# Reordering block 0's transposes and fill-in products in a fused attention and FFN kernel

## The chip, the cores and the metric

The kernel runs on one NeuronCore of a Trainium2 chip. The metric is the device time of one execution in microseconds (us), and the time of a kernel is the median over its runs. A profile of one execution comes with it: its times count from the start of the span, the stretch from the first to the last instruction.

The engines are named as in the profile: PE does matrix products and transposes (PEld is its weight loads), DVE and ACT are the vector and the scalar engine, POOL and SP here mostly issue transfers. PE writes only PSUM, which has eight banks of 128 x 512 fp32; ACT and DVE copy from there to SBUF.

## The reference

Linear ("lightning") attention with a decay for each head, followed by a gated FFN on its output. There are 4 batches, 8 heads, 768 positions and a head width of 64; d_model is 512, d_ff 1536.

```python
for b in range(nb):                                   # blocks of 64 positions
    intra = einsum('bhic,bhjc->bhij', qb, kb) * Dmask
    intra = einsum('bhij,bhjd->bhid', intra, vb)
    inter = einsum('bhid,bhde->bhie', qb * lam_pow, kv_state)
    out[:, :, sl] = intra + inter
    kv_state = lam_block * kv_state + einsum('bhsd,bhse->bhde', kb * rev_pow, vb)
x = out as (batch * seq, heads * head_dim)
y = (sigmoid(x @ w_gate) * (x @ w_val)) @ w_out
```

## The kernel before

The sequence is cut into six blocks of 128 positions, numbered n = 0 to 5. For each block the attention of all four batches gives `XT` (d_model by 512 tokens, bf16), and the FFN runs over it: `gp` and `vp` (L553) are the gate and value products, twelve tiles of d_ff each, `po` (L585) the output product. All matrix operands are bf16. In the steady part the attention of block n+1 is slipped between the FFN's products of block n by a written plan (`plan`, L672 on). The schedule is manual: each engine runs its instructions in the order in which the program lists them.

The change lies in block 0, which has no earlier FFN to hide behind. It has no incoming state, so its attention is scores, mask and output alone. Its list stands at L601 to L636. For each batch b:

- `t_0("k", b)` and `t_0("q", b)` (L285) transpose k and q on PE, eight small transposes each, into a PSUM tile `tk` or `tq`. For batches 0 and 1, k comes as fp32 (`h`) by two early loads and is cast on DVE (`cast_hw`, L358); everything else is loaded with a cast by POOL's queue.
- `e_k` (L353) and `e_q` (L340) copy these tiles to SBUF as `KS` and `QS`. ACT makes all the copies but that of `QS` of batch 0, which is DVE's.
- `s_0(b)` (L295) makes the scores in two PSUM banks `sp`, sixteen matmuls of 64 x 64 weights by 128 columns; DVE multiplies each bank with the decay mask (`MT`, L302), so there are eight such operations in all.
- `a_0(b)` (L311) multiplies with v into a bank `op`, and ACT copies it to `XT` (L318); for batch 3 the bank is split in two halves, and ACT and DVE copy one each.

The FFN's first products of tile 0 are taken in two halves (batches 0 and 1, then 2 and 3), so that they may start on the first half of `XT`.

Between these steps stand fill-in products, `zeros(m)` (L599): m matmuls of a zeroed tile with itself, 512 bf16 columns each, into a bank `zps` that nobody reads. There are eleven ahead of the first transpose and ten in between.

PSUM is shared by two pools: `ps_at` (five banks, tag "ps") for attention and `ps_ff` (three, tag "ff") for the FFN. A pool hands its banks round in turn, so a new tile waits until the last reader of the bank's tile of before is done. In the list before, each batch's `tk` and `tq` has a bank of its own, and `tk` of batches 2 and 3 lies in the FFN's pool, which also holds `zps`.

Of the kernel before, what the change touches and what calls it, by code (L numbers as in the profile page):

```python
# [8 lines left out]
FP32 = mybir.dt.float32  # L9
BF16 = mybir.dt.bfloat16  # L10
AF = mybir.ActivationFunctionType
ALU = mybir.AluOpType
# [4 lines left out]
def kernel(  # L17
# [11 lines left out]
    nc = tc.nc  # L29

    B, H, S, D = q.shape
    C = 128
    NSTEP = S // C
    HP = H // 2
    DM = H * D
# [11 lines left out]
    trsb = ctx.enter_context(tc.tile_pool(name="trsb", bufs=3))  # L47
# [6 lines left out]
    ps_at = ctx.enter_context(tc.tile_pool(name="ps_at", bufs=5, space=bass.MemoryType.PSUM))  # L54
    ps_ff = ctx.enter_context(tc.tile_pool(name="ps_ff", bufs=3, space=bass.MemoryType.PSUM))
# [19 lines left out]
    def swapped(n, b):  # L75
        return n > 0 and b >= NB2
# [7 lines left out]
    def rows_of(u):  # L84
        return slice(u * 64, (u + 1) * 64)
# [67 lines left out]
    ST, CP, XD = {}, {}, {}  # L153
# [50 lines left out]
    lamq, lamqs = lamq2[:, 0], lamq2[:, 1]  # L204
# [15 lines left out]
    def powers(w):  # L220
        nc.scalar.activation(mask0[:, w], mask0[:, w], AF.Exp)
# [47 lines left out]
    QS, KS, MT, XT, SP, OP = {}, {}, {}, {}, {}, {}  # L269
    QT, KT = {}, {}  # L270
    tqs, tks = {}, {}
# [5 lines left out]
                nc.tensor.transpose(ps[:, i, hp, :], T_[c, n][:, b, 2 * hp:2 * hp + 2, :], ident)  # L277
        (tqs if c == "q" else tks)[n, bs[0]] = ps

    def t_0(c, b, pool=ps_at, tag="ps"):  # L280
        ps = pool.tile([128, 1, HP, C], BF16, name="t" + c, tag=tag)
        for a in range(2):
            for e in range(2):
                for w in range(2):
                    nc.tensor.transpose(ps[rows_of(w), 0, 2 * a + e, :],  # L285
                                        T_[c, 0][:, b, 2 * (2 * a + w) + e, :], ident)
        (tqs if c == "q" else tks)[0, b] = ps

    def s_0(b):
        sp = [ps_at.tile([128, HP, C], FP32, name=f"sp{w}", tag="ps") for w in range(2)]  # L290
        for a in range(2):
            for e in range(2):
                for w in range(2):
                    for g in range(2):
                        nc.tensor.matmul(sp[w][rows_of(g), 2 * a + e, :],  # L295
                                         lhsT=KS[0, b][rows_of(w), 2 * a + e, rows_of(g)],
                                         rhs=QS[0, b][rows_of(w), 2 * a:2 * a + 2, rows_of(g)],
                                         start=(a == 0 and e == 0), stop=(a == 1 and e == 1),
                                         skip_group_check=True)
        MT[0, b] = mtp.tile([128, 2, HP, C], BF16, tag="MT", name="MT")  # L300
        for w in range(2):
            nc.vector.tensor_tensor(out=MT[0, b][:, w], in0=sp[w], in1=mask0[:, w], op=ALU.mult)  # L302

    def a_0(b, engs):
        n = len(engs)
        ops = [ps_at.tile([128, HP // n, C], FP32, name="op", tag="ps") for _ in range(n)]
        for r in range(HP):
            for e in range(2):
                for g in range(2):
                    o, i = divmod(r, HP // n)  # L310
                    nc.tensor.matmul(ops[o][rows_of(g), i, :], lhsT=T_["v", 0][rows_of(g), b, 2 * r + e, :],  # L311
                                     rhs=MT[0, b][rows_of(g), r % 2, 2 * (r // 2) + e, :],
                                     start=(i == 0 and e == 0), stop=(i == HP // n - 1 and e == 1),
                                     skip_group_check=True)
        if b == 0:
            new_xt(0)
        for o, eng in enumerate(engs):
            (eng.tensor_copy if eng is nc.vector else eng.copy)(  # L318
                XT[0][:, b // 2, o * (HP // n):(o + 1) * (HP // n), b % 2 * C:(b % 2 + 1) * C], ops[o])
# [12 lines left out]
        for bp in range(2):  # L332
            nc.scalar.copy(ST[1, 0][:, bp], cp[bp])

    def e_q(n, bs, eng=None):
        w = len(bs)
        src = tqs[n, bs[0]] if n < FIRST_XBAR else QT[n][:, bs[0]:bs[0] + w]
        t = trsb.tile([128, 2, HP, C], BF16, tag="QS", name="QS")
        if n == 0:
            (nc.scalar.copy if eng is nc.scalar else nc.vector.tensor_copy)(t[:, :w], src)  # L340
        else:
            nc.vector.tensor_tensor(
                out=t[:, :w], in0=src,
                in1=(lamqs if swapped(n, bs[0]) else lamq).unsqueeze(1).to_broadcast([128, w, HP, C]),
                op=ALU.mult)
        for i in range(w):
            QS[n, bs[i]] = t[:, i]

    def e_k(n, bs, parts=1):
        t = trsb.tile([128, 2, HP, C], BF16, tag="KS", name="KS")  # L350
        w = len(bs) // parts
        for i in range(parts):
            nc.scalar.copy(t[:, i * w:(i + 1) * w], tks[n, bs[0]][:, i * w:(i + 1) * w])  # L353
        for i in range(len(bs)):
            KS[n, bs[i]] = t[:, i]

    def cast_hw(b):
        nc.vector.tensor_copy(T_["k", 0][:, b], H32[:, b])  # L358
# [52 lines left out]
    def new_xt(n):  # L411
        XT[n] = xtp.tile([128, 2, NMT, TCH // 2], BF16, tag="XT", name="XT")
# [181 lines left out]

    zps = ps_ff.tile([128, DM], FP32, name="zps", tag="ff")

    def zeros(m):
        for _ in range(m):
            nc.tensor.matmul(zps, lhsT=ST[1, 0][:, 0, 0], rhs=ST[1, 0][:, 0], start=True, stop=True)  # L599

    exponents(0)  # L601
    powers(0)
    exponents(1)
    powers(1)
    zeros(11)
    cast_hw(0)
    cast_hw(1)
    t_0("k", 0)
    e_k(0, [0])
    zeros(1)  # L610
    t_0("k", 1)
    t_0("q", 0)
    e_q(0, [0], nc.vector)
    e_k(0, [1])
    t_0("q", 1)
    e_q(0, [1], nc.scalar)
    zeros(1)
    s_0(0)
    zeros(1)
    s_0(1)  # L620
    for b in range(2, 4):
        t_0("k", b, ps_ff, "ff")
        e_k(0, [b])
    zeros(3)
    for b in range(2, 4):
        t_0("q", b)
        e_q(0, [b], nc.scalar)
    zeros(1)
    s_0(2)
    a_0(0, (nc.scalar,))  # L630
    s_0(3)
    a_0(1, (nc.scalar,))
    zeros(2)
    a_0(2, (nc.scalar,))
    zeros(1)
    a_0(3, (nc.scalar, nc.vector))  # L636


# [183 lines left out]
```

## Time and profile before

| | |
|---|---|
| median of 4 runs | 225.37 us (225.08 to 225.67) |
| the profiled execution | 225.08 us, span 223.3 us |
| PE busy in the span | 216.8 us (97%) |
| DVE, ACT, POOL busy | 103.2, 108.6, 63.5 us |
| PE busy, 0 to 6.66 us | 4.77 of 6.66 |
| PE busy, 6.66 to 9.50 us | 2.58 of 2.84 |
| PE busy, 9.50 to 15.66 us | 5.44 of 6.16 |
| PE busy, 15.66 us to the end | 204.01 of 207.64 |

A line of the timeline gives the start in us, the busy time, the engine, the line of the kernel, the operation, what it writes and reads, the shape, the count, and in brackets the idle time of the engine before it with what ended it. The chain of waits follows the work that ended last back from the last instruction. Ends of matmuls are modelled, so their starts are the better measure; and a few matmul records can be missing (the page counts 18 fill-in products where the list has 21). A fill-in product counts as busy like any other.

### The profile page before, as it was taken

What the parts mean: (1) busy time and instruction counts of PE and PEld (TensorE: products, weight loads), DVE (VectorE), ACT (ScalarE), POOL (GpSimd) and SP (SyncE); (2) the same over time, 40 slices, a digit from 0 to 9 for tenths busy, and PEclk for the clock granted to TensorE, in tenths of its full rate; (3) what the DMA queues carried; (4) which work ended last, traced back from release to release, by engine and by line L of the source; (5) the groups of instructions that cost most, each with busy time, mean ns of one, the idle gap of its engine ahead of it and who ended that gap; (6) DMA issues with size and microseconds to landing.
All of it is one profiled execution on the core that took longest, in us unless ns stands there. A gap on an engine that the chain in (4) does not pass through costs nothing.

```text
span 223.3 us, 5470 instructions
## 1 busy us (share of the span) xinstructions
PE 216.8 (97%) x2310; PEld 107.7 (48%) x2321; DVE 103.2 (46%) x191; ACT 108.6 (49%) x237; POOL 63.5 (28%) x85
## 2 busy tenths in 40 slices
PE   7889999999999999999999999999999999999994
PEld 2565444557444544444544444544444544444443
DVE  4754565539777600785700686700676400333300
ACT  5757764494384523385433376342366342333221
POOL 7999855740291009302920030000000000000000
PEclk9999999999999999999999999999999999999999
DMA  6999999999899999997999986012100012100022
GB/s 116 175 179 187 196 199 183 165 156 167 127 96 157 267 217 120 175 132 163 95 158 178 234 58 41 3 50 94 47 3 0 3 48 96 47 0 1 3 94 95
DMA packets 99401, 25.27 MB, mean 113 GB/s; under 512 B 90032, under 2 KB 96432, under 8 KB 99376
## 3 DMA queue, kind: packets, MB, share of 16 engines
q0 software_dynamic: 77872, 13.90, 77.8%
q1 hardware_dynamic: 20688, 10.69, 19.4%
q10 hardware_dynamic: 816, 0.33, 0.6%
q8 instruction: 18, 0.29, 0.5%
q14 instruction: 7, 0.06, 0.1%
HBM read 28.32 MB, written 6.29 MB: 155 GB/s over the span
## 4 chain that ended last, share of the span: by engine, by line
PE 95%; DMA 2%; issue 1%; DVE 1%; ACT 0%; ACTq 0%; DVEq 0%
PE gp L553 28%; PE po L585 28%; PE vp L553 28%; DMA h<-in_k_dram 2%; PE sp L449 1%; PE cp L509 1%; PE op L473 1%; PE op L487 1%; PE zps L599 1%; PE op L311 1%; PE tk L285 1%; PE sp L295 1%; PE sp L375 0%; PE op L406 0%; PE tq L277 0%
## 5 line engine op out<-in xcount | busy, mean ns | idle before, releaser
L543 DVE SCALAR_TENSOR_TENSOR ht<-sg,vp 128x512 bf16<-128x512 f32 x72 | 49.5, 687 | 93.3 <-PE vp L553 88.5
L553 PE MATMUL gp<-XT,WG 128*128 128x512 bf16 (+1 forms) x296 | 74.3, 374 | 0.0
L553 PE MATMUL vp<-XT,WV 128*128 128x512 bf16 (+1 forms) x296 | 74.3, 373 | 0.0
L563 ACT ACTIVATE sg<-gp 128x512 f32<-128x512 f32 x72 | 43.0, 597 | 59.2 <-PE gp L553 59.2
L585 PE MATMUL po<-WO,ht 128*128 128x512 bf16 (+2 forms) x292 | 63.5, 370 | 0.7 <-issue 0.2
L553 PEld LDWEIGHTS <-WV 128*128 128x128 bf16 x296 | 29.0, 98 | 33.2
L585 PEld LDWEIGHTS <-ht 128*128 128x128 bf16 x300 | 28.2, 98 | 32.2 <-issue 0.4
L553 PEld LDWEIGHTS <-WG 128*128 128x128 bf16 x296 | 28.2, 98 | 31.3
L589 ACT ACTIVATE ob<-po 128x512 f32<-128x512 f32 (+1 forms) x24 | 14.0, 583 | 38.9 <-PE po L585 38.9
L143 ACT ACTIVATE kd<-kb,kds 128x128 bf16<-128x128 bf16 x80 | 25.2, 390 | 0.0
L661 POOL COPY gates<-qt 128x1 bf16<-128x1 bf16 x4 | 0.7, 186 | 50.2 <-DMA qt<-qb 50.2
L499 ACT CAST XT<-op 128x512 bf16<-128x512 f32 x16 | 8.2, 599 | 5.0 <-PE op L487 5.0
L459 DVE TENSOR_TENSOR MT<-sp,mask 128x512 bf16<-128x512 f32 x16 | 10.3, 682 | 0.0
L96 POOL DMA_DIRECT2D vb<-in_v_dram x6 | 9.0, 1501 | 3.2 <-issue 1.6
L102 POOL DMA_DIRECT2D qb<-in_q_dram x10 | 8.8, 893 | 3.2 <-DMA WO<-in_moe_w_out_dram 3.2
L102 POOL DMA_DIRECT2D kb<-in_k_dram x10 | 9.0, 920 | 1.0 <-DMA WG<-in_moe_w_gate_dram 0.5
L599 PE MATMUL zps<-st 128*128 128x512 bf16 x18 | 7.1, 530 | 1.7 <-DVE st L174 1.5
L121 POOL DMA_DIRECT2D WV<-in_moe_w_val_dram x9 | 7.4, 840 | 0.3 <-DMA WG<-in_moe_w_gate_dram 0.3
L118 POOL DMA_DIRECT2D WG<-in_moe_w_gate_dram x8 | 6.8, 856 | 0.0
L534 DVE SCALAR_TENSOR_TENSOR st<-st,pow_l,cp 128x128 bf16<-128x128 bf16 x24 | 6.7, 342 | 0.0
L96 POOL DMA_DIRECT2D kb<-in_k_dram x5 | 5.9, 1185 | 0.9 <-DMA WG<-in_moe_w_gate_dram 0.9
L353 ACT COPY KS<-tk 128x512 bf16<-128x512 bf16 (+1 forms) x6 | 4.3, 728 | 3.6 <-PE tk L277 2.1
(91 smaller groups left out, 126.7 us busy)
## 6 DMA issues: line engine op xcount, KB each, us to landing
out_dram<-ob SPq DMA_DIRECT2D x19, 256.0 KB, 2.0
vb<-in_v_dram POOLq DMA_DIRECT2D x4, 512.0 KB, 7.2
qb<-in_q_dram POOLq DMA_DIRECT2D x14, 128.0 KB, 7.6
kb<-in_k_dram POOLq DMA_DIRECT2D x12, 128.0 KB, 9.0
WO<-in_moe_w_out_dram POOLq DMA_DIRECT2D x4, 384.0 KB, 12.0
kb<-in_k_dram POOLq DMA_DIRECT2D x5, 256.0 KB, 9.4
qb<-in_q_dram POOLq DMA_DIRECT2D x5, 256.0 KB, 9.1
WG<-in_moe_w_gate_dram POOLq DMA_DIRECT2D x4, 256.0 KB, 7.0
```

The costliest lines, as they stand in the source:

```text
L96: nc.gpsimd.dma_start(out=T_[c, n][:, b0:nat], in_=src[b0:nat, :, sl, :].rearrange("b h s d -> s (b h) d"))
L102: nc.gpsimd.dma_start(out=T_[c, n][:, m:b1, u::2, :], in_=src[m:b1, 1 - u::2, sl, :].rearrange("b h s d -> s (b h) d"))
L121: nc.gpsimd.dma_start(out=WV[:, :, f0 * 128:f1 * 128], in_=wv_r[:, :, f0 * 128:f1 * 128])
L143: nc.scalar.mul(KD[n][:, at, i, :], T_["k", n][:, at, i, :], kds[:, min(n // FIRST_XBAR, 1), h:h + 1])
L459: nc.vector.tensor_tensor(out=MT[n, bp][:, u], in0=SP[n, bp][u], in1=mask[:, u ^ bp].unsqueeze(1).to_broadcast([128, 2, HP, L]), op=ALU.mult)
L499: nc.scalar.copy(XT[n][:, bp].rearrange("p m (j c i) -> p m j c i", j=2, c=2)[:, :, :, c, :], OP[n, c, bp])
L543: return nc.vector.scalar_tensor_tensor(out=o, in0=g, scalar=1.0, in1=x, op0=ALU.add, op1=ALU.mult)
L553: nc.tensor.matmul(ps[:, part], lhsT=W[:, mt, fs], rhs=XT[n][:, part, mt], start=(part is not second and mt == 0), stop=(part is not first ...
L563: nc.scalar.activation(sg, gp.rearrange("p a b -> p (a b)"), AF.Tanh, scale=0.5)
L585: nc.tensor.matmul(po[:, :c1 - c0], lhsT=HT[n, ft][:, tt * 128:(tt + 1) * 128], rhs=WO[:, ft, c0:c1], start=(ft == 0), stop=(ft == NFT - 1))
L589: (eng.mul if eng is nc.scalar else eng.tensor_scalar_mul)(o, po[:, :c1 - c0], 0.5)
L599: nc.tensor.matmul(zps, lhsT=ST[1, 0][:, 0, 0], rhs=ST[1, 0][:, 0], start=True, stop=True)
```

## The change

- q of a batch is transposed right behind its k: in the list k0, q0, k1, q1, where k0, k1, q0, q1 stood.
- The transposed k of two batches share one PSUM bank, one half each, and so do the transposed q. All of them lie in `ps_at`.
- The copies of block 0 have a function of their own, `e_0`. DVE copies `QS` of batches 0 and 1, ACT the rest.
- For batches 2 and 3 the order is k2, k3, q2, scores 2, q3, output 0, scores 3, output 1; q3 stood ahead of scores 2.
- The outputs of batches 0 and 1 go to banks of the FFN's pool.
- The fill-in products read the same zeroed tile as fp32. Three of 512 columns stand at the start, where eleven were; one of 384 ahead of q2 and one of 256 behind it; the others are gone.

```diff
-    def t_0(c, b, pool=ps_at, tag="ps"):
-        ps = pool.tile([128, 1, HP, C], BF16, name="t" + c, tag=tag)
+    def t_0(c, b):
+        ts = tqs if c == "q" else tks
+        if b % 2 == 0:
+            ts[0, b] = ps_at.tile([128, 2, HP, C], BF16, name="t" + c, tag="ps")
+        ps = ts[0, b & ~1]
         for a in range(2):
             for e in range(2):
                 for w in range(2):
-                    nc.tensor.transpose(ps[rows_of(w), 0, 2 * a + e, :],
+                    nc.tensor.transpose(ps[rows_of(w), b % 2, 2 * a + e, :],
                                         T_[c, 0][:, b, 2 * (2 * a + w) + e, :], ident)
-        (tqs if c == "q" else tks)[0, b] = ps
+        ts[0, b] = ps
...
-    def a_0(b, engs):
+    def a_0(b, engs, pool=ps_at, tag="ps"):
         n = len(engs)
-        ops = [ps_at.tile([128, HP // n, C], FP32, name="op", tag="ps") for _ in range(n)]
+        ops = [pool.tile([128, HP // n, C], FP32, name="op", tag=tag) for _ in range(n)]
...
+    def e_0(c, b, eng):
+        es = QS if c == "q" else KS
+        if b % 2 == 0:
+            t = trsb.tile([128, 2, HP, C], BF16, tag=c.upper() + "S", name=c.upper() + "S")
+            for i in range(2):
+                es[0, b + i] = t[:, i]
+        (nc.scalar.copy if eng is nc.scalar else nc.vector.tensor_copy)(
+            es[0, b], (tqs if c == "q" else tks)[0, b][:, b % 2])
...
-    def zeros(m):
+    nought = ST[1, 0].rearrange("p a h j d -> p (a h j d)").bitcast(FP32)
+
+    def zeros(m, w=DM):
         for _ in range(m):
-            nc.tensor.matmul(zps, lhsT=ST[1, 0][:, 0, 0], rhs=ST[1, 0][:, 0], start=True, stop=True)
+            nc.tensor.matmul(zps[:, 0:w], lhsT=nought[:, 0:128], rhs=nought[:, 0:w], start=True, stop=True)
...
-    zeros(11)
+    zeros(3)
     cast_hw(0)
     cast_hw(1)
     t_0("k", 0)
-    e_k(0, [0])
-    zeros(1)
+    e_0("k", 0, nc.scalar)
+    t_0("q", 0)
+    e_0("q", 0, nc.vector)
     t_0("k", 1)
-    t_0("q", 0)
-    e_q(0, [0], nc.vector)
-    e_k(0, [1])
+    e_0("k", 1, nc.scalar)
     t_0("q", 1)
-    e_q(0, [1], nc.scalar)
-    zeros(1)
+    e_0("q", 1, nc.vector)
     s_0(0)
-    zeros(1)
     s_0(1)
     for b in range(2, 4):
-        t_0("k", b, ps_ff, "ff")
-        e_k(0, [b])
-    zeros(3)
-    for b in range(2, 4):
-        t_0("q", b)
-        e_q(0, [b], nc.scalar)
-    zeros(1)
+        t_0("k", b)
+        e_0("k", b, nc.scalar)
+    zeros(1, 384)
+    t_0("q", 2)
+    e_0("q", 2, nc.scalar)
+    zeros(1, 256)
     s_0(2)
-    a_0(0, (nc.scalar,))
+    t_0("q", 3)
+    e_0("q", 3, nc.scalar)
+    a_0(0, (nc.scalar,), ps_ff, "ff")
     s_0(3)
-    a_0(1, (nc.scalar,))
-    zeros(2)
+    a_0(1, (nc.scalar,), ps_ff, "ff")
     a_0(2, (nc.scalar,))
-    zeros(1)
     a_0(3, (nc.scalar, nc.vector))
```

More of the change, by code (lines that the diff above doesn't have):

```diff
@@ L333, in c_0, with e_q @@
             nc.scalar.copy(ST[1, 0][:, bp], cp[bp])
-    def e_q(n, bs, eng=None):
+    def e_0(c, b, eng):
[6 more added lines that the diff above has]
+            es[0, b], (tqs if c == "q" else tks)[0, b][:, b % 2])
+    def e_q(n, bs):
         w = len(bs)
@@ L338, in e_q, with e_k @@
         t = trsb.tile([128, 2, HP, C], BF16, tag="QS", name="QS")
[L339 to L345, printed above, removed]
+        nc.vector.tensor_tensor(
+            out=t[:, :w], in0=src,
+            in1=(lamqs if swapped(n, bs[0]) else lamq).unsqueeze(1).to_broadcast([128, w, HP, C]),
+            op=ALU.mult)
         for i in range(w):
             QS[n, bs[i]] = t[:, i]
-    def e_k(n, bs, parts=1):
+    def e_k(n, bs):
         t = trsb.tile([128, 2, HP, C], BF16, tag="KS", name="KS")
-        w = len(bs) // parts
-        for i in range(parts):
-            nc.scalar.copy(t[:, i * w:(i + 1) * w], tks[n, bs[0]][:, i * w:(i + 1) * w])
+        nc.scalar.copy(t, tks[n, bs[0]])
         for i in range(len(bs)):
```

## The prediction

> **What bounds the kernel now.** I read the page first, then its chain of waits in order of time, then the timeline of the first 18 us. From the page, busy shares and the chain:
>
> ```profile
> PE 216.8 (97%) x2310; PEld 107.7 (48%) x2321; DVE 103.2 (46%) x191; ACT 108.6 (49%) x237; POOL 63.5 (28%) x85
> PE 95%; DMA 2%; issue 1%; DVE 1%; ACT 0%; ACTq 0%; DVEq 0%
> ```
>
> PE is the bound of the whole. The waits of PE after 15.6 us hold a single entry, 0.2 us at `po`, so whatever moves the first FFN product (`gp`, 15.67 us) moves the end by as much. The change touches only what lies ahead of that product. There PE is busy with fill-ins; the chain shows what decides:
>
> ```profile
> 10.14 0.75 PE zps L599 x3
> 10.90 0.36 PE tq L285 x8
> 11.26 0.02 issue
> 11.28 0.59 ACT QS L340
> 11.88 0.04 issue
> 11.92 0.47 PE sp L295 x16
> 12.39 0.68 DVE MT L302
> ```
>
> Columns: start, duration, what. The scores of batch 2 (`sp`, 11.92) wait for ACT's copy of its transposed q; DVE's masking (`MT`) waits for the scores. The timeline holds the durations that I use:
>
> ```profile
> 1.53 4.77 PE L599 MATMUL zps<-st 128*128 128x512 bf16 x11 [1.53 <-DVE st L174]
> 6.18 0.92 DVE L358 CAST kb<-h 128x512 bf16<-128x512 f32 x2 [0.17 <-DMA h<-in_k_dram]
> 7.12 1.25 ACT L353 COPY KS<-tk 128x512 bf16<-128x512 bf16 x2 [0.33 <-PE tk L285]
> 8.01 0.42 DVE L340 COPY QS<-tq 128x512 bf16<-128x512 bf16 x1 [0.91 <-PE tq L285]
> 9.01 2.48 DVE L302 TENSOR_TENSOR MT<-sp,mask 128x512 bf16<-128x512 f32 x4 [0.57 <-PE sp L295]
> 9.51 0.64 PE L285 MATMUL tk<-ident,kb 128*64 128x128 bf16 x16
> 9.96 1.07 ACT L353 COPY KS<-tk 128x512 bf16<-128x512 bf16 x2 [1.10 <-PE tk L285]
> 10.07 0.82 PE L599 MATMUL zps<-st 128*128 128x512 bf16 x3
> 12.37 2.48 DVE L302 TENSOR_TENSOR MT<-sp,mask 128x512 bf16<-128x512 f32 x4 [0.88 <-PE sp L295]
> 14.78 0.39 PE L599 MATMUL zps<-st 128*128 128x512 bf16 x1
> 15.10 0.63 PE L311 MATMUL op<-MT,vb 64*64 64x128 bf16 x16
> 15.67 0.61 PE L553 MATMUL gp<-XT,WG 128*128 128x256 bf16 x4
> ```
>
> Columns: start, busy time, engine, line, operation, count, idle time before it. DVE masks eight times 0.6 us, in two runs of four with 0.88 us idle between. The second run ends at 14.85, the last output product starts at 15.10 (the fill-in of 14.78 holds it for 0.25), the FFN at 15.67. So the start of the FFN is the end of DVE's second run plus 0.8 us, and that run starts 0.45 after the scores of batch 2.
>
> **Small prices.** A released PE instruction starts 0.05 after its releaser (QS ends 11.87, `sp` 11.92). Eight transposes (one batch) start over 0.20 us and deliver after 0.41; a copy follows 0.04 later and takes 0.59 on ACT, 0.42 on DVE. PE changes tile shape 0.15 after the last start. A bf16 fill-in of 512 columns holds the next shape for 0.32 (14.78 to 15.10): 0.22 of streaming and 0.10 more.
>
> **The change, step by step.**
>
> Opening fill-ins: eleven bf16 products cost 4.77, 0.43 each, and end before the cast of k allows the first transpose (6.18 + 0.43 + 0.05 = 6.66). Three fp32 products take their place. No row shows fp32 on PE. From below: one bf16 price each, 1.3 us, which ends at 2.8 and leaves PE idle to 6.66. From above: an fp32 number split in two halves makes four part products, each with its own visible weight load (0.15): 3 x 4 x 0.58 = 7.0, end 8.5, which would hold the transposes for 1.9. I take four parts with loads hidden, as in the x11 row: 3 x 4 x 0.43 = 5.1, end 6.65, cost 0 to 0.15.
>
> Batches 0 and 1: k0 at 6.66; q0 next. Its second load, issued at 2.06, lands at about 7.05 (4.5 to 5.2 from issue), so q0 at 7.15, and DVE copies it 7.6 to 8.03. As the changed program is built, k1 waits for the copy of k0, since both now lie in one bank: 7.70 + 0.05, its copy 8.2 to 8.8. q1 waits for DVE's copy of q0: 8.08, its copy 8.53 to 8.96, now on DVE. Scores of batch 0 at 8.42 (8.49 before), of batch 1 at 9.01 (9.15 before, where a fill-in held them). The first mask can't start before QS1 leaves DVE at 8.96: 9.0, as before. The gain of 0.14 ends there; DVE's first run still ends at 11.49.
>
> Batches 2 and 3: k2 at 9.36, copied 9.81 to 10.40. Before, k3 followed k2 at once in another bank (x16 in 0.64). Now k3 shares its bank and waits for that copy: 10.45, 0.7 later than before. Behind it on PE stand the 384-column fill-in, q2, the 256-column one and the scores of batch 2, all held. ACT copies k3 10.9 to 11.5. The fill-in begins at 10.8. Price from below 0.16 (one bf16 pass over 384 columns) + 0.10; from above four passes with open loads, 4 x (0.16 + 0.10) + 0.10 = 1.14; taken: 4 x 0.16 + 0.10 = 0.75, nearest to the row of three zps that it replaces (0.82 busy). So q2 at 11.54 (10.83 before), copied 12.0 to 12.6. The 256-column fill-in (4 x 0.11 + 0.10 = 0.54 by the same price, 0.2 to 0.9 by the bounds) runs 11.88 to 12.42 under that copy: nothing, up to 0.2 at its upper price. Scores of batch 2 at 12.63, against 11.92: +0.71.
>
> The Trainium skill, "FP8 and Floating Point Precision", section "TensorE Precision Notes", has true fp32 at four passes through the array; by that alone the 384-column product streams 0.64 us, and no run here shows it.
>
> Batch 3: q3 now stands behind those scores, at 12.98, copied 13.43 to 14.02, scores of batch 3 at 14.07. DVE masks batch 2 from 13.08 and could take batch 3 at 14.29, but its scores come at 14.52: 0.23 more. DVE's second run ends at 15.80, against 14.85: +0.95. Given back: no fill-in stands before the last output product (-0.25), and four of its sixteen matmuls need only the mask before the last one and have run by then (-0.05). The FFN starts at 16.3 against 15.67: **+0.65**.
>
> At no cost: the first two outputs in the FFN's banks. They remove a wait for the copy of batch 0's output (ACT, ended 13.40), which wasn't last; `gp` now waits for the output copy of batch 1, at 15.6, under the last output product. One copy leaves ACT (0.59) and one joins DVE (0.42); both lie in gaps. POOL's and SP's queues are the same and wait for nothing that moved, so every load lands as before; the loads of q2, q3 (10.0) and v (11.5) are early enough.
>
> **Sum.** The profiled execution took 225.08 with a span of 223.3, the fast end of the runs; the median is 225.37. On the first +0.65 gives 225.7, on the median **226.0**, which I take. With the fill-in at its bounds: from below q2's copy waits for ACT to finish k3, scores 12.15, FFN +0.2; from above q2 at 11.93 and the second fill-in until 13.2, FFN +1.2. The opening's upper bound would come on top (+1.9); I leave it out of the range, since in the x11 row every weight load lies under a product.
>
> **PE's clock.** The x11 row runs at 0.43 per 512 columns and the x3 row at 0.22: PE runs at half pace until about 6 us, at full pace from then, while the page's granted clock reads 9 throughout. Of the ten fill-ins after 6.7 us in the list two are left, so PE idles more: 7.4 to 7.75, 9.6 to 10.45 and 15.2 to 15.85 are the longest gaps. The skill's "TensorE: Matmul & The Clock Gate", Part 1, ties half pace to an idle window of 3.4 us. By it none of these gaps costs anything; its Part 4 has transposes not counted as busy, which speaks against this change. The trace of before shows no fall of pace after 6 us, so the fall is a rival and not a term.
>
> **Rivals.**
> 1. PE falls to half pace in the thinned stretch. For it: the start shows that the pace isn't free. Against: fill-ins of 0.6 and 0.4 remain. From 9.5 to 12.9 the fill-in of 384 grows by 0.64 and the three sets of transposes by 0.2 each: +1.2 on top, 227.2; if it lasts a few us into the FFN, another 1.5.
> 2. Faster: DVE's idle 0.88 closes. The place is the scores of batch 2: if they start by 10.95, the second mask run follows the first at once, and with the fill-in of 14.78 gone the FFN starts 0.9 to 1.1 earlier: 224.4. It decides if q2 is transposed by 9.9 and copied ahead of k3. Against: q2 stands behind k3, which waits for ACT until 10.4, and its load lands only at 10.0.
> 3. Little happens: fp32 fill-ins cost one bf16 pass and the clock holds: +0.2, 225.6.
>
> **How the numbers follow.** Forecast (+0.4 to +1.2) 0.60, rival 1 0.13, rival 2 with lesser forms of it 0.12, rival 3 0.15. The band of 0.2% is 0.45 us, about what a measurement of this kernel tells from none; executions before spread over 0.6. Rival 3 and the low edge of the forecast (0.11) fall into it: same 0.26, faster 0.12, slower 0.62. The range leaves out rival 2 and the longest form of rival 1: 225.0 to 227.2.
>
> **What would show it.** Right: k3's transposes at 10.4, a gap of half a microsecond between the two KS copies, scores of batch 2 past 12.4, DVE's idle before the second mask run near 1.6, `gp` at 16.2 to 16.5, nothing changed behind it. Wrong: a 384-column fill-in far from 0.65 us, transposes at twice their time after 7 us (rival 1), or a second mask run that follows the first at once (rival 2).

## The result and the profile after

The changed kernel takes 225.62 us (median of 36 runs, 225.50 to 225.96); the kernel before, beside it, 225.13 us (57 runs, 224.78 to 225.67). The ratio is 1.0022, 95% interval 1.0018 to 1.0027: slower by 0.49 us. The profiled execution of the changed kernel took 225.59 us with a span of 223.8.

The page of the changed kernel, busy shares and the chain by engine:

```profile
PE 216.8 (97%) x2302; PEld 108.3 (48%) x2310; DVE 103.6 (46%) x192; ACT 108.2 (48%) x236; POOL 63.5 (28%) x85
PE 93%; DMA 2%; ACT 1%; DVE 1%; issue 1%; ACTq 0%; DVEq 0%
```

PE's busy time is what it was, though the fill-ins became fewer: the one of 384 fp32 columns alone counts as busy for 0.91 us. PE's share of the chain fell from 95% to 93%, and ACT's rose from 0 to 1%. Where that is, the timeline tells (start, busy time, engine, line, operation, count, idle time before it; the lines that matter):

```profile
9.42 0.41 PE L288 MATMUL tk<-ident,kb 128*64 128x128 bf16 x8
9.88 0.59 ACT L344 COPY KS<-tk 128x512 bf16<-128x512 bf16 x1 [1.11 <-PE tk L288]
10.52 0.41 PE L288 MATMUL tk<-ident,kb 128*64 128x128 bf16 x8 [0.68 <-ACT KS L344]
10.86 0.91 PE L608 MATMUL zps<-st 128*128 128x384 f32 x2
10.97 0.59 ACT L344 COPY KS<-tk 128x512 bf16<-128x512 bf16 x1 [0.50 <-PE tk L288]
11.70 0.41 PE L288 MATMUL tq<-ident,qb 128*64 128x128 bf16 x8
12.16 0.59 ACT L344 COPY QS<-tq 128x512 bf16<-128x512 bf16 x1 [0.61 <-PE tq L288]
12.80 0.42 PE L298 MATMUL sp<-QS,KS 64*64 64x128 bf16 x16
13.24 1.29 DVE L305 TENSOR_TENSOR MT<-sp,mask 128x512 bf16<-128x512 f32 x2 [1.75 <-PE sp L298]
14.68 1.29 DVE L305 TENSOR_TENSOR MT<-sp,mask 128x512 bf16<-128x512 f32 x2 [0.15 <-PE sp L298]
16.48 0.61 PE L560 MATMUL gp<-XT,WG 128*128 128x256 bf16 x4
```

PE idles 0.68 us ahead of k3's transposes, and the bracket names ACT's copy of k2, the other half of the same bank. The fill-in, q2, its copy, the scores of batch 2 and the masks follow in a line. DVE, idle 0.88 between its two mask runs before, is idle for 1.75, and once more for 0.15. The FFN starts at 16.48, 0.81 later than before, though the execution is only half a microsecond longer.

The other part lies 100 us further on. These are two copies of FFN outputs that follow each other on ACT, before (with PE's weight loads between them) and after:

```profile
113.28 0.60 ACT L589 ACTIVATE ob<-po 128x512 f32<-128x512 f32 x1 [0.92 <-PE po L585]
115.75 2.25 PEld L585 LDWEIGHTS <-ht 128*128 128x128 bf16 x11 [0.42 <-issue]
116.17 0.60 ACT L589 ACTIVATE ob<-po 128x512 f32<-128x512 f32 x1 [2.29 <-PE po L585]
```

```profile
114.09 0.60 ACT L596 ACTIVATE ob<-po 128x512 f32<-128x512 f32 x1 [0.91 <-PE po L592]
116.69 0.60 ACT L596 ACTIVATE ob<-po 128x512 f32<-128x512 f32 x1 [1.99 <-PE po L592]
```

2.89 us apart before, 2.60 after. In the trace of before PE stands still for 0.30 us between two `po` matmuls (they start at 115.23 and 115.75, 0.52 apart, where others are 0.216 apart), and the weight load of the second comes late with nothing named but "issue". The stretch from the first `gp` to the end is 207.64 us before and 207.32 after. So +0.81 - 0.32 = +0.49, and the spans, rounded, differ by 0.5.

### The profile page after: what moved, and what is told of

Read it like the earlier page. It is cut to its first block, busy times and chain, and to the rows that moved or that the text cites. A ratio compares the mean times of both kernels' runs of the same rounds, so it can differ in the third digit from the quotient of the medians.

```text
span 223.8 us, 5450 instructions
## 1 busy us (share of the span) xinstructions
PE 216.8 (97%) x2302; PEld 108.3 (48%) x2310; DVE 103.6 (46%) x192; ACT 108.2 (48%) x236; POOL 63.5 (28%) x85
## 4 chain that ended last, share of the span: by engine, by line
PE 93%; DMA 2%; ACT 1%; DVE 1%; issue 1%; ACTq 0%; DVEq 0%
PE gp L560 28%; PE po L592 28%; PE vp L560 28%; DMA h<-in_k_dram 2%; PE sp L456 1%; PE cp L516 1%; PE op L480 1%; PE op L494 1%; PE tk L288 1%; PE sp L298 1%; DVE MT L305 1%; ACT QS L344 1%; ACT KS L344 1%; PE tq L288 1%; PE sp L382 0%
## 5 line engine op out<-in xcount | busy, mean ns | idle before, releaser
L466 DVE TENSOR_TENSOR MT<-sp,mask 128x512 bf16<-128x512 f32 x16 | 10.3, 682 | 0.0
L608 PE MATMUL zps<-st 128*128 128x512 f32 (+2 forms) x10 | 6.3, 763 | 1.5 <-DVE st L174 1.5
L305 DVE TENSOR_TENSOR MT<-sp,mask 128x512 bf16<-128x512 f32 x8 | 5.1, 684 | 1.9 <-PE sp L298 1.9
```

The lines of the kernel that those rows point to most:

```text
L466: nc.vector.tensor_tensor(out=MT[n, bp][:, u], in0=SP[n, bp][u], in1=mask[:, u ^ bp].unsqueeze(1).to_broadcast([128, 2, HP, L]), op=ALU.mult)
```

## The experiments

My theory by then: the shared bank (k3 waits for ACT) and the 384-column fill-in add up to the later FFN, and the stall at `po` is a matter of its own. Times are medians; ratios are against the kernel before on the same chip, whose median there was 225.03 to 225.12 us. The experiments ran on several chips, so differences of 0.1 us between two of them say little.

**e1, own banks for k2 and k3**

```diff
+        if c == "k" and b >= 2:
+            ts[0, b] = ps_ff.tile([128, 2, HP, C], BF16, name="t" + c, tag="ff")
+            ps = ts[0, b]
```

> The changed kernel, but the transposed k of batches 2 and 3 lie in a bank of their own each, in the FFN's pool, as before. Theory (the shared bank makes k3 wait for ACT's copy of k2, and everything behind k3 on PE is held): k3 starts at 9.65 us in place of 10.51, the scores of batch 2 at 11.8 in place of 12.79, the FFN (gp) at 15.45 in place of 16.48; 1.0 us faster than the changed kernel, near 224.6, 0.2 under the kernel before at the FFN. Rival (the fp32 fill-in ahead of q2 is the delay, the bank is not): k3 earlier, but scores and FFN by 0.2 us at most, about 225.4.

224.84 us, ratio 0.9985 (0.9976 to 0.9995): 0.8 under the changed kernel, where 1.0 was expected. PE transposes both in one run again:

```profile
9.77 0.64 PE L292 MATMUL tk<-ident,kb 128*64 128x128 bf16 x16
12.27 0.42 PE L302 MATMUL sp<-QS,KS 64*64 64x128 bf16 x16
15.95 0.61 PE L564 MATMUL gp<-XT,WG 128*128 128x256 bf16 x4
```

The whole block stands 0.35 late in this profile (first mask at 9.36 in place of 9.01), since PE got its full clock only at 7.45 us and the first transposes ran at half pace. Less that, the scores stand at 11.92 (expected 11.8) and the FFN at 15.60 (15.45). The bank theory holds; the rival's 0.2 doesn't. The edit gives k2 and k3 a tile as well as a bank of their own, so it doesn't tell which of the two makes the program wait.

**e2, no fp32 fill-ins after the start** (`zeros(1, 384)` and `zeros(1, 256)` left out)

> The changed kernel without the two fp32 fill-ins of 384 and 256 columns. Theory (bank wait and fill-in add up): q2 at 10.76, its copy waits for ACT to finish k3 and runs 11.5 to 12.07, scores of batch 2 at 12.12 in place of 12.79, FFN at 15.8 in place of 16.48; 0.67 us faster than the changed kernel, near 224.95. Rival A (the fill-in alone is the delay): 0.8 us or more, FFN at 15.67 or earlier. Rival B (the fill-ins hold PE's pace): eight transposes start over 0.4 us in place of 0.2 after 10 us, first FFN products at 0.43 us per 512 columns, as slow as the changed kernel or slower by 0.5 and more.

225.40 us, ratio 1.0007 (0.9997 to 1.0018), in two groups: six of twelve runs between 224.94 and 225.21, six between 225.59 and 225.79. The six long ones have a mean granted clock of 0.992, the others 0.998 or 1.0. The profile is one of the long ones; its stretches, with length, busy time of PE, PEld, DVE, ACT and POOL, and granted clock (third from the end):

```profile
6.39:9.81 3.42, 2.99 (x73) 2.00 (x73) 2.34 (x6) 1.69 (x4) 3.42 (x6) 1.00 1.81 178
9.81:13.22 3.41, 1.79 (x57) 1.50 (x55) 2.37 (x5) 1.96 (x4) 3.41 (x5) 1.00 1.81 178
13.22:16.63 3.41, 3.38 (x72) 3.12 (x66) 1.92 (x4) 2.15 (x5) 3.41 (x9) 0.50 1.80 178
```

After a window of 3.41 us in which PE is busy for 1.79, the next runs at half the clock, and the FFN begins at 16.69 although the scores of batch 2 stood at 12.11 as expected. Both the theory and rival B are right: against the changed kernel 0.55 us is won where the clock holds (median of those six 225.06, near 224.95 expected), and where it doesn't, in half of the runs, all of that is lost again (225.66). Why it holds in one run and not in the next isn't shown; the edges of the windows lie elsewhere in each execution, so the thin stretch may fall into one window or be shared by two.

**e3, q3 ahead of the scores of batch 2**

```diff
     zeros(1, 256)
+    t_0("q", 3)
+    e_0("q", 3, nc.scalar)
     s_0(2)
-    t_0("q", 3)
-    e_0("q", 3, nc.scalar)
```

> The changed kernel with q3 transposed ahead of the scores of batch 2, as before. Theory: scores of batch 2 stay at 12.8, q3 is copied by 13.25, scores of batch 3 no longer keep DVE waiting between batch 2 and batch 3 (0.15 us idle, 14.53 to 14.68), FFN 0.2 to 0.25 earlier, at 16.25; about 225.4. Rival (the order of q3 costs nothing): FFN at 16.48, 225.6.

225.73 us, ratio 1.0027 (1.0017 to 1.0036): the theory missed, and so did the rival's unchanged FFN. The time is not clearly different from the changed kernel's, but the FFN starts at 16.60, 0.12 later.

```profile
12.81 0.41 PE L288 MATMUL tq<-ident,qb 128*64 128x128 bf16 x8
13.15 0.42 PE L298 MATMUL sp<-QS,KS 64*64 64x128 bf16 x16
```

q3 shares its bank with q2, so it waits for the copy of q2 (ends 12.75), and now it stands ahead of the scores, which go from 12.80 to 13.15. I had seen the shared bank for k and forgotten it for q. With shared banks, the order that the change chose is the better one, by these 0.12 us.

**e4, before without its three late fill-ins** (`zeros(2)` and `zeros(1)` ahead of the last two outputs left out)

> The kernel before without the three fill-ins ahead of the last two output products. Theory (the last of them holds the last output product after its mask is done): that product follows the mask of batch 3 by 0.05 us in place of 0.25, and a quarter of it runs ahead of the last mask, so the FFN starts 0.25 to 0.3 earlier, at 15.4; 0.3 us faster than before, about 224.85. Rival (they keep PE's pace into the FFN): granted clock at a half in some stretch after 13 us, no faster or slower than before.

224.53 us, ratio 0.9967 (0.9950 to 0.9984), clock 1.0 from 4.78 us on. The FFN is at the theory's place:

```profile
15.41 0.61 PE L553 MATMUL gp<-XT,WG 128*128 128x256 bf16 x4
```

The time fell by 0.56, twice what was expected. In the profiled executions 0.25 of that lies ahead of the FFN; the other 0.31 is the stall at `po`, which is gone (the two copies stand at 113.03 and 115.62, and from the FFN's start to the end it is 207.32 us).

**e5, before without all ten fill-ins in between**

> The kernel before without its ten fill-ins in between; the eleven at the start stay. Theory (fill-ins only occupy PE): q2 at 10.07, copied behind k3 on ACT, 10.95 to 11.55, scores of batch 2 at 11.6 in place of 11.92, last output product 0.25 earlier against its mask, FFN at 15.1 in place of 15.67; 0.55 us faster than before, near 224.6. Rival (they hold PE's pace): matmuls after 9.5 us at half pace, the FFN's first products 0.43 us per 512 columns, 1 to 3 us slower than before.

224.21 us, ratio 0.9960 (0.9948 to 0.9972): 0.9 under the kernel before, where 0.55 was expected. Clock 1.0 in all six runs. The FFN starts even at 14.69 (15.1 expected), because the early fill-ins no longer hold the transposes either: the first mask stands at 8.82 and k2 at 9.07 in place of 9.51. Of this, 0.13 is k's earlier arrival in that execution (k0 at 6.53). PE is busy for 2.70, 2.46 and 2.81 us in the windows of 3.41 from 6.11 on: that was enough, 1.79 in e2 was not. But the start is partly lost again, as the value product now waits for its weights:

```profile
14.69 0.61 PE L553 MATMUL gp<-XT,WG 128*128 128x256 bf16 x4
15.60 0.61 PE L553 MATMUL vp<-XT,WV 128*128 128x256 bf16 x4 [0.29 <-DMA WV<-in_moe_w_val_dram]
```

**e6, before with the fp32 opening alone**

```diff
+        if m == 11:
+            for _ in range(3):
+                nc.tensor.matmul(zps, lhsT=nought[:, 0:128], rhs=nought, start=True, stop=True)
+            return
```

> The kernel before with its eleven opening bf16 fill-ins replaced by three fp32 ones of 512 columns; all else as before. FFN start by the theory on fp32 (1.71 us each at half pace, 6.65 together): k0 at 6.65 or, where PE is released late, 6.95; FFN at 15.65 to 15.95. On the stall of 0.30 us that the profiled execution of before shows between two matmuls of po at 115.2 us and the changed kernel doesn't: theory A (it hangs on where instructions lie in PE's list, which is 21 rows shorter here): no stall, runs close together near 224.8, 0.3 under before. Theory B (it is chance or comes from transfers): runs spread as before, 224.8 to 225.7, median 225.1.

224.82 us, ratio 0.9977 (0.9956 to 0.9999), ten of twelve runs between 224.72 and 224.90. FFN at 15.75, no stall, 207.36 us from there to the end. So the opening costs the FFN next to nothing, and the stall left with a change at the very start of PE's list. That list is shorter by 10 rows as the profile records them (2316 weight loads and as many matmuls, where before has 2321 weight loads), not by the 21 of the expectation.

**e7, before once more**

> The kernel before once more, for a second profile. If the stall of 0.30 us at po (115.2 us) belongs to this list of instructions, it stands there again, or another of its size; if it was chance, the stretch from the first gp to the end is 207.33 us as in the other kernels' profiles, in place of 207.64.

225.29 us in its one run. The stall is there, at the same matmul (it and the one ahead of it start at 115.27 and 115.95), now 0.46 us long; 207.82 us from the FFN's start to the end.

**e8, own banks and no fp32 fill-ins after the start** (the edits of e1 and e2 together)

> The changed kernel with k of batches 2 and 3 in banks of their own and without the two fp32 fill-ins of 384 and 256 columns. Theory (the two costs add): k3 at 9.65, q2 at 10.07 when its load is in, its copy behind k3's on ACT until 11.46, scores of batch 2 at 11.5, FFN at 15.2 in place of 16.48; 1.3 us faster than the changed kernel, about 224.3. Rival (PE falls to half pace without the fill-ins): in some executions a stretch of 3.41 us at half the granted clock, and those take 0.6 us more.

224.51 us, ratio 0.9962 (0.9946 to 0.9979): 1.1 under the changed kernel, 1.3 expected. The profile again has the late clock (7.66 us, first mask at 9.36):

```profile
11.84 0.42 PE L302 MATMUL sp<-QS,KS 64*64 64x128 bf16 x16 [1.21 <-ACT QS L348]
15.53 0.61 PE L564 MATMUL gp<-XT,WG 128*128 128x256 bf16 x4
```

Less 0.35 the scores stand at 11.49 and the FFN at 15.18, both as expected. Against e1, late by the same, the fill-ins alone cost the FFN 0.42 (15.95 to 15.53). No run shows a mean clock near the 0.992 of e2's long ones.

**e9, e4 with PE's list as long as before's**

```diff
+    for _ in range(3):
+        nc.tensor.matmul(zps[rows_of(0), 0:64], lhsT=ST[1, 0][rows_of(0), 0, 0, 0], rhs=ST[1, 0][rows_of(0), 0, 0, 0],
+                         start=True, stop=True)
     a_0(3, (nc.scalar, nc.vector))
```

> The kernel of e4 (before, without the three late fill-ins) with three tiny matmuls of 64 x 64 columns in their place, which run while the last output product waits for its mask. PE's list is as long as before's again, and every later instruction has the place in it that it has there. Theory A (the stall at po near 115 us hangs on the instructions' places): FFN at 15.4 as in e4, but the stall of 0.3 to 0.45 is back, and the median is 224.85 to 225.0 in place of 224.53, spread as before. Theory B (the stall has to do with the time at which po is reached, or with chance): no stall, 224.55.

224.81 us, ratio 0.9988 (0.9979 to 0.9998), spread over 224.44 to 225.35: 0.28 above e4, with three more matmuls that run while PE waits anyway, and just under the 224.85 that theory A gave. The two copies of FFN outputs:

```profile
113.29 0.60 ACT L589 ACTIVATE ob<-po 128x512 f32<-128x512 f32 x1 [0.92 <-PE po L585]
116.05 0.60 ACT L589 ACTIVATE ob<-po 128x512 f32<-128x512 f32 x1 [2.17 <-PE po L585]
```

2.76 apart, against 2.59 in e4: the stall is back at its place, 0.17 long in this execution, shorter than expected. That is theory A. The time is the weaker sign: in this profile the full clock came only at 7.51 us, so the FFN starts at 15.68 and not at 15.4. Of the 0.43 us between the two profiled executions (224.95 and 224.52), 0.26 is that and 0.17 the stall; how the 0.28 between the medians divides isn't shown.

**e10, e5 with both gate halves ahead of the value product**

```diff
+            if n == 0:
+                order = [(gp, WG, first), (gp, WG, second), (vp, WV, whole)]
```

> The kernel of e5 (before, without the ten fill-ins in between) with the FFN's first tile of block 0 in the order gate half, gate half, whole value product, since in e5 the value product waited 0.47 us for its weights (WV), which land by 15.55. Theory: gp at 14.7, second half at 15.25 when XT is whole, vp at 15.7 with no wait or 0.1; 0.3 us faster than e5, about 223.9. Rival (the wait only moves, to XT's second half or to the weights of the next tile): 224.2 as e5.

224.03 us (five runs, 223.80 to 224.04), ratio 0.9947 (0.9933 to 0.9961). `vp` starts at 15.80, 0.1 after the gate. It is the fastest version found: 1.0 us under before, 1.6 under the changed kernel. Against e5 it is 0.2 us, where 0.3 was expected, and the two intervals overlap.

**e11, bf16 in place of the two later fp32 fill-ins** (three of 512 columns for the one of 384, two for the one of 256)

> The changed kernel with three bf16 fill-ins of 512 columns in place of the fp32 one of 384 and two in place of the one of 256: as many columns by four passes. Theory (fp32 costs four passes and about 0.1 us of open weight load): q2 0.1 earlier than in the changed kernel, at 11.6, FFN at 16.4, 0.1 us faster, about 225.5. Rival (fp32 products are the main cost): FFN 0.3 us earlier or more.

225.58 us, ratio 1.0018 (1.0008 to 1.0028), FFN at 16.41: 0.07 earlier than in the changed kernel, as the theory has it; the time itself can't tell 0.1 us. fp32 as such is not the cost; the time that the fill-ins hold PE is.

## Why the prediction was right, and where not

**The cause** was as forecast: k3 waits for the copy of k2 in the bank that they share, at 10.52 (10.45 forecast), and everything behind it on PE is held. e1 and e8 show it by taking the sharing away. The two halves of the bank are one tile of the program, and both edits separate tile and bank together, so which of the two makes the program as built wait is open.

**The path** follows the working step by step: q0 7.22 (7.15), k1 7.74 (7.75), first mask 9.01 (9.0), k2 9.42 (9.36), q2 11.70 (11.54), scores of batch 2 at 12.80 (12.63), of batch 3 at 14.24 (14.07), FFN 16.48 (16.3). The FFN moved by 0.81, not 0.65. The mis-sized term is the 384-column fill-in: 0.84 us (10.86 to 11.70), not 0.75. Each fp32 product shows as two records, and the second starts 0.43 after the first at full clock (10.86 and 11.29): 0.32 for two passes of 384 columns, by the 0.216 that a bf16 product of 512 columns takes, and 0.10 more, as long as a bf16 weight load in these profiles. I had taken all weight loads as hidden after the x11 row, which ran at half clock. In the opening of the changed kernel, at half clock too, the records of 512 columns stand 0.85 apart, two passes of 0.43, with nothing open. The rest of the difference is q0's 0.07, which runs through to the end. The four passes that the Trainium skill gives for true fp32 ("FP8 and Floating Point Precision", "TensorE Precision Notes") agree with these records.

**Where it failed:** "nothing changed behind" the FFN's start. The step that whatever moves the first FFN product moves the end by as much did not hold: that product moved by 0.81, the end by 0.49. The prediction had no term for the stall at `po`. The 0.2 us of "issue" that it read among PE's waits is another entry, at 49.55 us, and stands in the changed kernel's profile too (50.36); the stall of 0.30 us at 115 us isn't in that list at all and shows only in the spacing of the matmuls, in the weight load behind it and in the copies on ACT. e6, e4 and e9 show that it goes with the places of the instructions in PE's list: 10 rows fewer at the start (e6) or 6 fewer before the FFN (e4) take it away, and three tiny matmuls that restore the length (e9) bring it back. It stands in all three profiles of lists as long as before's (2321 weight loads), at the same matmul, 0.17 to 0.46 us long, and in none of the ten others. The time at which `po` is reached is not it: the first of the two copies stands at 113.29 in e9, which stalls, and at 113.37 in e6, which doesn't. The change's list has 22 rows fewer (2310 weight loads, each with its matmul) and gets back 0.3 us by that, nothing that its text is about.

The forecast of 226.0 was 0.4 too high, by three misses that partly cancel: 0.24 because I set the sum on a median of four runs, 225.37, which over 57 runs is 225.13; 0.3 for the stall; and 0.16 the other way for the FFN's start. That 226.0 came no further off is in part luck.

**Rival 1** is real but didn't strike: the changed kernel's profile keeps its clock after the release, and its runs have mean clocks of 0.998 to 1.0; without its two fill-ins (e2) half of the runs lost it. The rule of the Trainium skill of no idle gaps on PE above about 3.4 us ("TensorE: Matmul & The Clock Gate", Part 1) has the length of the window right, 3.41 us in e2, but doesn't cover what happened there: no gap in e2 was above 1.0 us, and the clock fell after a window that was 52% busy. The prediction's worry that transposes may not count as busy is not borne out: without them that window of e2 has 0.83 us of work, and the one of e8 from 7.66 us has 0.83 too, but with them it is 1.79 against 2.44, and e8 kept its clock. **Rival 2** stayed away for the reasons given. e5 and e10 come near it by other means, without sharing and fill-ins: DVE's idle time shrinks to 0.39 and 0.40, and the FFN starts at 14.69 and 14.79. **Rival 3**, one pass for fp32, is excluded by the 0.84.

What remains of the change without shared k banks and fill-ins gained nothing here: e5 and e8 both have no fill-ins behind the opening, and e5, in the old order, starts the FFN at 14.82 (with k0 set to 6.66), e8, in the new one, at 15.18 (less its late clock).

Open: what makes PE stall at that place. An 8 KB transfer of an instruction queue starts at 114.7 us in before, but at 114.6 and 114.8 in e4 and e6, which don't stall; and one of 16 KB of another instruction queue at 113.4 in before, but at 113.0 and 113.4 in those two. So neither transfer alone is it.

## What to carry to other kernels

A bank shared by the transposes of two batches saves a bank, but where a reader on another engine stands between its two writers, the second writer waits for that reader (0.68 us of idle PE here), and with it all that is queued behind it. Read fill-in products as occupants of the engine: price each by how long it holds the next instruction, and take them out one place at a time with the granted clock of each window beside it. And compare the stretches that a change doesn't touch, too: here 0.3 us, more than a third of what block 0 lost, came back there with an instruction list that became shorter.

## What the runs showed of the hardware

- PE's full clock came at 4.68 (e11), 4.78 (e4), 5.30 (after), 6.08 (before), 7.45 (e1) and 7.66 us (e8), with PE busy from 1.53 in all of them. A release at 7.45 or 7.66 moved the first mask by 0.35 us (9.36, where the changed kernel has 9.01).
- In e2 the clock rose at 6.39, fell at 13.22 and rose at 16.63 us: two windows of 3.41 us and one. The window with PE busy for 1.79 us was followed by half clock; those with 2.44 to 2.56 (e5, e8, the changed kernel) were not. Transposes are part of these busy times, and without them e2's and e8's would be alike.
- A stall of 0.17 to 0.46 us on PE goes with the place of instructions in its list, 100 us behind the edit; its cause is open.
